# A spectral filter beside a token MLP: the first two pairs' step to token frequencies in one visit to the array's quarters

## Chip, cores and metric

The kernel runs on one core of one Trainium2 chip. The metric is the device time of one execution in microseconds; for the kernel before, the median of three runs is 366.05 us (365.9 to 366.07).

## The reference, cut to what matters

```python
x = A_x                                   # (1, 2048 tokens, 512 channels)
xn = layernorm(x)                         # over the channels
X = rfft2(xn) * (w_r + 1j * w_i)          # over tokens and channels
s = irfft2(X, (2048, 512))                # the global filter
u = gelu(einsum("bsd,sf->bdf", layernorm(xn), w1) + b1)    # w1: 2048 x 1792, over the tokens
y = einsum("bdf,fs->bds", u, w2) + b2
return x + s * silu(y.transpose(0, 2, 1))
```

All is float32. The large products (w1 and w2) are made of three products of rounded parts: each factor is split into a high part (a rounded copy) and a low part (the difference).

## The kernel before, in words

The work has three stages. In the first, the 16 blocks of 128 tokens are normalised, half of the hidden products are summed into six PSUM banks, and a first part of the token transform is written to `ey`, which holds its results by 16 low frequencies, `eyl(lo)`. In the second stage, which the change touches, TensorE goes through the rest of the hidden products (`hidden_rest`, rows `h..,w1e..` and `h..,w1h..`/`w1l..` of the profile), and between them through eight filter steps, each for a pair of low frequencies (`filter_pair`). In the third stage come the products with w2, the inverse transforms and the output.

One pair n goes through `filter_pair` in pieces, each ended by a `yield`:

1. load the table gf (`c_g[n]`);
2. and 3. twice: transform over the channels (rows `cd,ey`, four matmuls into bank 6 or 5), and a copy by ScalarE to `sh`, the pair's signals;
4. the way to token frequencies: four matmuls `sh,gf` of 64 rows into 64 columns, one in each quarter of the array (the profile shows two records for each matmul of this type, so eight), into banks 6 and 5; the load of hf (`c_h[n]`); two copies by ScalarE to `here`, a half of the tile `xc`; two transfers by GpSimd that write the other half, `there`, with the partitions swapped; and on GpSimd's queue two loads of filter weights `wt` (a ring of three buffers);
5. on VectorE: two small products `s1`, two scalings of 128x1024, four products of 128x512 with the weights;
6. on VectorE: a sum of 128x1024, two of 128x512, and a small one into `here` from `s1`;
7. the way back: 32 matmuls `hf,xc` in the array's quarters (64 records), which read `here`, and two copies to `ey`.

Which piece stands where among the hidden products is set in the loop over n at the end of the stage: `advance` takes a list in which a number is so many groups of hidden products (three matmuls each), `None` is a step that splits a part of the finished hidden layer (tiles `fa`, `fb`, `fc`, `fd`, `u`), and a pair of numbers `(k, piece)` takes the k-th of the filter generators one piece on. The order of pairs is `[1, 2, 0, 3, 4, 5, 6, 7]`: the first one's tiles carry the number 1 (`sh1`, `xc1`, `hf1`), the second's 2, the third's 0. In one such turn, pair n passes pieces 2 to 4, pair n-1 its VectorE work, and pair n-2 its way back just ahead of pair n's piece 4, so that two quarter steps are neighbours from the third pair on.

TensorE's matmuls and GpSimd's transfers keep the program's order. The order of the other engines is made when the program is built, by a list scheduler with the program's order as priority and costs of its own. Tiles of one tag share a ring of buffers; a load into one waits until its last reader is done. `w1_part` splits the hidden layer's weights (`w1s` into `w1h` on ScalarE and `w1l` on VectorE).

Of the kernel before, what the change touches and what calls it, by code (L numbers as in the profile page):

```python
# [9 lines left out]
F32 = mybir.dt.float32  # L10
F32R = mybir.dt.float32r
AF = mybir.ActivationFunctionType
# [3 lines left out]
P = 128  # L16
S, D, F = 2048, 512, 1792
# [124 lines left out]
def spectral_mixer_kernel(tc, x, w1, b1, w2, b2, wk, we, wx, c_f, c_ft, c_d, c_i, c_g, c_h, out):  # L142
    nc = tc.nc
    V, A, G, T, SY = nc.vector, nc.scalar, nc.gpsimd, nc.tensor, nc.sync

    def pool(stack, side, name, bufs):
        return stack.enter_context(tc.tile_pool(name=name, bufs=bufs, side=side, reuse_waits="tile"))
# [14 lines left out]
    with tc.tile_pool(name="ps", bufs=1, space=PSUM) as psp, ExitStack() as left, ExitStack() as right:  # L162
        ps = psp.tile([P, 8, 512], F32, name="ps")
# [161 lines left out]
        def w1_tiles(j):  # L325
            return [[w1r.tile([P, NE1 * P], F32R, name=f"w1{n}{a}_{j}", tag=f"w1{n}{a}", bufs=3) for n in "hl"] for a in range(2)]
# [134 lines left out]
        T = Kept(T, keep)  # L461
# [22 lines left out]
        w = w1_tiles(0)  # L484
# [23 lines left out]
        for j in range(NJ):  # L508
# [26 lines left out]
            if more:  # L535
                w = w1_tiles(j + 1)
# [84 lines left out]
        mp = pool(rstage, "right", "mid", 2)  # L621
# [9 lines left out]
        def eyl(lo):  # L631
            return ey.rearrange("p b (l h) j c -> p l b (h j c)", h=4)[:, lo]

        def filter_pair(n):

            gf = mp.tile([P, 2, 64], F32, name=f"gf{n}", tag="gf")
            SY.dma_start(gf, c_g[n])
            yield
            sh = []
            for l in range(2):  # L640
                pd = ps[:, 6 - l]
                for b in range(4):
                    T.matmul(pd[:, b * P:(b + 1) * P], eyl(2 * n + l)[:, b], cd[:, b], start=True, stop=True)
                sh.append(mp.tile([P, D], F32, name=f"sh{n}_{l}", tag="sh"))
                A.activation(sh[l], pd, AF.Copy)
                yield

            if n == 0:

                for l in range(2):  # L650
                    SY.dma_start(eyl(l)[:2], wx[:, 2 * l:2 * l + 2].rearrange("p k (b c) -> p (k b) c", c=P))
            for l in range(2):
                for t in range(2):
                    rows = slice(64 * t, 64 * t + 64)
                    T.matmul(ps[64 * l:64 * l + 64, 6 - t], gf[rows, l], sh[l][rows],
                             start=True, stop=True)

            hf = mp.tile([P, 2, 2, 64], F32, name=f"hf{n}", tag="hf")
            SY.dma_start(hf, c_h[n])


            xc = mp.tile([P, 2, 2, 2, 256], F32, name=f"xc{n}", tag="xc")
            there, here = xc[:, 0], xc[:, 1]
            for t in range(2):
                A.activation(here[:, :, t], ps[:, 6 - t].rearrange("p (s c) -> p s c", s=2), AF.Copy)  # L665
            for c in range(2):
                keep(G.dma_start(*(v.rearrange("p s t c -> p s (t c)") for v in (there[c::2], here[1 - c::2, ::-1]))))  # L667
            if n == 0:
                for to, signal, b in ((0, 0, 0), (1, 1, 1), (3, 0, 2), (2, 1, 2)):
                    V.tensor_mul(room(both, to), here[both, signal, 0].rearrange("p (h c) -> p h c", h=2), room(both, b))  # L670
            wt = wts.pop(), weights(2 * n + 1)
            if n != order[-1]:
                wts.append(weights(2 * order[order.index(n) + 1]))
            yield
            s1 = mp.tile([P, 2, 2, 2], F32, name=f"s1_{n}", tag="s1")
            k1, k2 = (e[:, 2 * n:2 * n + 2].rearrange("p t s -> p s t") for e in (e1, e2))
            V.tensor_mul(s1[:, 0], here[:, :, :, 0], k2)
            V.tensor_mul(s1[:, 1], there[:, ::-1, :, 0], k1)
            av, bv = (v.rearrange("p s t c -> p s (t c)") for v in (here, there))
            V.scalar_tensor_tensor(av, bv, turn[:, 0:1], av, op0=ALU.mult, op1=ALU.add)  # L680
            V.scalar_tensor_tensor(bv, bv, turn[:, 1:2], av, op0=ALU.mult, op1=ALU.subtract)
            for t in range(2):
                V.tensor_mul(here[:, :, t], here[:, :, t], wt[t][:, ::3])
                V.tensor_mul(there[:, :, t], there[:, :, t], wt[t][:, 1:3])
            yield
            V.tensor_add(there, there, here[:, ::-1])
            V.tensor_sub(here[:, 0], there[:, 1], there[:, 0])
            V.tensor_add(here[:, 1], there[:, 1], there[:, 0])
            V.tensor_add(here[:, :, :, 0], s1[:, 0], s1[:, 1])
            if n == 0:  # L690
                for s, op, (a, b) in ((0, V.tensor_sub, (0, 2)), (1, V.tensor_add, (1, 3))):
                    op(here[both, s, 0].rearrange("p (h c) -> p h c", h=2), room(both, a), room(both, b))
            yield

            po = [ps[:, bank].rearrange("p (b t c) -> p b t c", b=4, t=2) for bank in ((5, 6) if n == order[-2] else (3, 4))]
            for t in range(2):
                for b in range(4):
                    s = b // 2
                    for k in range(2):
                        c = 128 * (b % 2) + 64 * k  # L700
                        for l in range(2):
                            rows = slice(64 * l, 64 * l + 64)
                            T.matmul(po[l][64 * k:64 * k + 64, b, t], here[rows, s, t, c:c + 64], hf[rows, t, s],
                                     start=True, stop=True)
            for l in range(2):
                if n == order[-1]:
                    last_copies.append((eyl(2 * n + l), po[l].rearrange("p b t c -> p b (t c)")))
                else:
                    A.activation(eyl(2 * n + l), po[l].rearrange("p b t c -> p b (t c)"), AF.Copy)
            yield  # L710
# [3 lines left out]
        def room(rows, k):  # L714

            return eyl(k // 2)[rows, 2 * (k % 2):2 * (k % 2) + 2]

        def weights(i):
            wt = mp.tile([P, 4, 256], F32, name=f"wt{i}", tag="wt", bufs=WT)
            keep(G.dma_start(wt, wk[:, i]))  # L720
            return wt
# [5 lines left out]
        def form_step():  # L727

            while todo and held[0] + 2 <= passed[0]:
                if next(todo[0], "end") != "end":  # L730
                    return
                todo.pop(0)
# [29 lines left out]
        order = [1, 2, 0, 3, 4, 5, 6, 7]  # L762
        wts = [weights(2 * order[0])]
        filters = [filter_pair(n) for n in order]
        rest = hidden_rest()

        def advance(work):

            for what in work:
                if what is None:  # L770
                    form_step()
                elif isinstance(what, int):
                    for _ in range(what):
                        next(rest)
                else:
                    next(filters[what[0]])
# [8 lines left out]
        for n in range(8):  # L785
            a, b, c, d, e, f = PACE[n]
            u, v, w = ([None] * (k < MADE[n]) for k in range(3))
            advance([(n - 1, 5)] * (n > 0) + [(n, 1), a] + u + [(n, 2)] + [(n + 1, 0)] * (n < 7) + [b])
            advance([(n - 2, 6)] * (n > 1) + [(n, 3), c] + v + [d, (n, 4), e] + w + [f])
        advance([(7, 5), *LAST, (6, 6), (7, 6)])  # L790
        run(rest)
        passed[0] = NV + NJ
# [144 lines left out]
        V, A, SY, G = (Kept(e, keep) for e in (nc.vector, nc.scalar, nc.sync, nc.gpsimd))  # L937
# [209 lines left out]
```

## Time and profile before

| | |
|---|---|
| median of the runs | 366.05 us |
| the profiled execution | 366.06 us |
| its span, first to last instruction | 364.3 us |
| TensorE busy | 357.9 us, 98% |
| VectorE busy | 305.9 us, 84% |
| ScalarE busy | 211.2 us, 58% |
| GpSimd busy | 87.1 us, 24% |
| granted TensorE clock | 0.999 |

How to read it: PE is TensorE's matmuls, PEld its weight loads, DVE VectorE, ACT ScalarE, POOL GpSimd, SP SyncE. A row of the timeline has the start (us from the span's start), the length from the first start to the last end of the group, engine, line, operation, tiles out and in with their numbers left out, shape, count, and in brackets the idle time before it with what ended it. Matmuls overlap, so TensorE reads as busy throughout; a slower stage shows in the starts. A row of a queue (SPq, POOL with DMA) is the issue of transfers; when they land is told apart.

### The profile page before, as it was taken

To read this page: it belongs to the slowest core of one execution; us is meant where nothing else is said; L and a number is where in the kernel's file an instruction comes from. 1 tells how busy PE (TensorE), PEld (TensorE's weight loads), DVE (VectorE), ACT (ScalarE), POOL (GpSimd) and SP (SyncE) were. 2 spreads that over 40 slices of the span, in tenths; PEclk is the share of its full clock that TensorE was granted. 3 is DMA by queue.
4 is the path that set the end of the run, shared out by engine and by line. 5 is a ranking of instruction groups with operands and counts; after the bars stand their busy time and mean duration, and the time that the engine had idled before them with its cause. 6 is when DMAs were issued, how large, how long until landed. Compare 5 with 4: busy or idle time off the path is not lost.

```text
span 364.3 us, 8799 instructions
## 1 busy us (share of the span) xinstructions
PE 357.9 (98%) x3452; PEld 310.6 (85%) x3452; DVE 305.9 (84%) x587; ACT 211.2 (58%) x385; POOL 87.1 (24%) x134
## 2 busy tenths in 40 slices
PE   8999999999999999999999999999999999999994
PEld 7788888888777778777888999989898989898983
DVE  4899999967799996999995988687887969696984
ACT  3887788857534426755237875555464546565441
POOL 4233333323222012220111001040403223140330
PEclk9999999999999999999999999999999999999999
DMA  7978999306695596896568288688888989897724
GB/s 211 245 188 199 218 279 315 160 0 161 184 237 202 190 261 177 244 241 199 175 222 171 101 228 176 187 175 204 185 187 211 172 231 158 233 161 216 124 28 89
DMA packets 33293, 68.66 MB, mean 188 GB/s; under 512 B 4612, under 2 KB 19380, under 8 KB 33124
## 3 DMA queue, kind: packets, MB, share of 16 engines
q1 hardware_dynamic: 24276, 42.44, 42.0%
q0 software_dynamic: 8496, 25.01, 32.2%
q10 hardware_dynamic: 480, 0.66, 0.6%
q8 instruction: 27, 0.44, 0.5%
q14 instruction: 14, 0.11, 0.1%
HBM read 59.70 MB, written 8.13 MB: 186 GB/s over the span
## 4 chain that ended last, share of the span: by engine, by line
PE 97%; DMA 1%; ACT 0%; DVE 0%; ACTq 0%; issue 0%; DVEq 0%
PE ps L139 97%; DMA w1r<-in_w_dram 1%; DVE rows L139 0%; ACTq L452 0%; ACT w1h L466 0%; ACT g L139 0%; DVEq L1143 0%
## 5 line engine op out<-in xcount | busy, mean ns | idle before, releaser
L139 PE MATMUL ps<-h,w1h 128*128 128x512 f32 x400 | 116.5, 398 | 0.0
L139 PEld LDWEIGHTS ps<-h,w1h 128*128 128x128 f32 x400 | 72.9, 188 | 19.9 <-issue 4.9
L139 PE MATMUL ps<-h,w1l 128*128 128x512 f32 x200 | 67.6, 390 | 0.0
L139 DVE TENSOR_TENSOR w2f<-a,w2f 128x896 fp32r<-128x896 f32 x36 | 39.2, 1090 | 21.6 <-ACT w2f L139 21.6
L139 PEld LDWEIGHTS ps<-h,w1l 128*128 128x128 f32 x200 | 37.6, 188 | 8.1
L139 ACT ACTIVATE w2f<-a 128x896 fp32r<-128x896 f32 x36 | 36.8, 1023 | 12.8 <-PE ps L139 7.5
L139 PE MATMUL ps<-fb,w2f 128*128 128x256 f32 x336 | 41.9, 280 | 0.0
L139 POOL DMA_DIRECT2D s<-in_w_dram x14 | 18.4, 1311 | 96.1 <-DVE c L139 46.4
L139 PE MATMUL ps<-fa,w2f 128*128 128x256 f32 x336 | 41.3, 278 | 0.0
L139 PEld LDWEIGHTS ps<-fb,w2f 128*128 128x128 f32 x336 | 39.7, 188 | 0.9 <-issue 0.8
L139 PE MATMUL ps<-fc,w2f 128*128 128x256 f32 x336 | 39.9, 278 | 0.0
L139 PEld LDWEIGHTS ps<-fa,w2f 128*128 128x128 f32 x336 | 39.8, 188 | 0.0
L139 PEld LDWEIGHTS ps<-fc,w2f 128*128 128x128 f32 x336 | 39.2, 188 | 0.0
L139 POOL DMA_DIRECT2D out_dram<-r x28 | 23.6, 1278 | 27.5 <-DVE r L139 27.5
L155 ACT ACTIVATE w1h<-w1s 128x512 fp32r<-128x512 f32 x26 | 16.2, 632 | 23.7 <-PE ps L139 11.7
L667 POOL DMA_DIRECT2D xc<-xc x16 | 9.8, 620 | 70.3 <-ACT xc L665 55.1
L308 POOL TENSOR_TENSOR ey<-t 128x256 f32<-128x256 f32 x16 | 15.7, 978 | 44.0 <-DVE t L306 44.0
L139 ACT ACTIVATE w2f<-s 128x896 fp32r<-128x896 f32 x15 | 15.3, 1023 | 13.8 <-PE ps L139 12.4
L469 DVE TENSOR_TENSOR w1l<-w1r,w1h 128x384 fp32r<-128x384 f32 x32 | 21.3, 670 | 0.0
L139 PE MATMUL ps<-fd,w2f 128*128 128x256 f32 x168 | 20.7, 278 | 0.0
L139 ACT ACTIVATE g<-c,b2t 128x256 f32<-128x256 f32 x24 | 12.1, 505 | 14.6 <-DVE c L139 14.6
L268 ACT ACTIVATE h<-x,nbm,rsm 128x256 f32<-128x256 f32 (+1 forms) x34 | 18.4, 591 | 3.6 <-DVE nbm L263 3.0
(134 smaller groups left out, 605.7 us busy)
## 6 DMA issues: line engine op xcount, KB each, us to landing
a<-in_w_dram SPq DMA_DIRECT2D x22, 448.0 KB, 4.1
wt<-in_wk_dram POOLq DMA_DIRECT2D x16, 512.0 KB, 5.9
s<-in_w_dram SPq DMA_DIRECT2D x16, 448.0 KB, 4.5
s<-in_w_dram POOLq DMA_DIRECT2D x16, 448.0 KB, 6.8
w1s<-in_w_dram SPq DMA_DIRECT2D x52, 128.0 KB, 5.0
w1r<-in_w_dram SPq DMA_DIRECT2D x28, 192.0 KB, 4.7
xc<-xc POOLq DMA_DIRECT2D x16, 256.0 KB, 3.0
out_dram<-in_x_dram SPq DMA_DIRECT2D x4, 960.0 KB, 6.5
```

The costliest lines, as they stand in the source:

```text
L139: return lambda *args, **kw: self.keep(operation(*args, **kw))
L155: return A.activation(hi, src, AF.Copy), V.tensor_sub(lo, src, hi.bitcast(F32))
L268: keep(A.activation(to, v, AF.Identity, bias=m["nb"][:, i], scale=m["rs"][:, i, 1:2]))
L308: G.tensor_add(ey[:, 0::3, :, j], a, b)
L469: keep(V.tensor_sub(dst, src, hi.bitcast(F32)))
L667: keep(G.dma_start(*(v.rearrange("p s t c -> p s (t c)") for v in (there[c::2], here[1 - c::2, ::-1]))))
```

## The change

The first pair's visit to the quarters is taken away from its place, and its four matmuls stand in one visit with the second pair's, at the second pair's place. Its signals stay meanwhile in a buffer of tag xc (`shs`) in place of two of tag sh, and its results go to banks 4 and 3 in place of 6 and 5. What follows on the visit (copies, transfers, weight loads, VectorE's pieces) moves with it: the first pair's piece 5 stands after the second pair's visit, piece 6 ahead of the third pair's first channel transform, side by side with the second pair's piece 5. The way back of the first pair stays where it was.

```diff
+            top = 4 if n == order[0] else 6
...
-            sh = []
+            sh, first = [], n == order[0]
+            if first:
+                shs = mp.tile([P, 2, 2, 2, 256], F32, name=f"shs{n}", tag="xc")
...
-                sh.append(mp.tile([P, D], F32, name=f"sh{n}_{l}", tag="sh"))
+                sh.append(shs[:, 0, l].rearrange("p s c -> p (s c)") if first else mp.tile([P, D], F32, name=f"sh{n}_{l}", tag="sh"))
...
-                    T.matmul(ps[64 * l:64 * l + 64, 6 - t], gf[rows, l], sh[l][rows],
+                    T.matmul(ps[64 * l:64 * l + 64, top - t], gf[rows, l], sh[l][rows],
...
-                A.activation(here[:, :, t], ps[:, 6 - t].rearrange("p (s c) -> p s c", s=2), AF.Copy)
+                A.activation(here[:, :, t], ps[:, top - t].rearrange("p (s c) -> p s c", s=2), AF.Copy)
...
-            advance([(n - 1, 5)] * (n > 0) + [(n, 1), a] + u + [(n, 2)] + [(n + 1, 0)] * (n < 7) + [b])
-            advance([(n - 2, 6)] * (n > 1) + [(n, 3), c] + v + [d, (n, 4), e] + w + [f])
+            advance([(0, 5)] * (n == 2) + [(n - 1, 5)] * (n > 1) + [(n, 1), a] + u + [(n, 2)] + [(n + 1, 0)] * (n < 7) + [b])
+            if n < 2:
+                advance([(0, 3)] * n + v + [(0, 4), (1, 3)] * n + [c, d] + [(1, 4)] * n + [e] + w + [f])
+            else:
+                advance([(n - 2, 6), (n, 3), c] + v + [d, (n, 4), e] + w + [f])
```

In the code the pieces count from 0: `(k, 3)` is piece 4 of the list above, `(k, 6)` the way back.

TensorE at the two visits, before (in the rows a tile's name carries the pair's or block's number, and last a buffer number):

```order
L139 MATMUL ps_58<-h1_83,w1e1_1018 128x512 x6
L139 MATMUL ps_58<-sh1_0_1418,gf1_1387 64x512 x2
L139 MATMUL ps_58<-sh1_1_1433,gf1_1387 64x512 x2
L139 MATMUL ps_58<-h2_84,w1e2_1109 128x512 x12
L139 MATMUL ps_58<-h3_85,w1e3_1166 128x512 x9
```
```order
L139 MATMUL ps_58<-h4_86,w1e4_1241 128x512 x6
L139 MATMUL ps_58<-sh2_0_1513,gf2_1435 64x512 x2
L139 MATMUL ps_58<-sh2_1_1536,gf2_1435 64x512 x2
L139 MATMUL ps_58<-h4_86,w1e4_1241 128x512 x3
```

and the same two places now:

```order
L139 MATMUL ps_58<-h1_83,w1e1_1018 128x512 x6
L139 MATMUL ps_58<-h2_84,w1e2_1109 128x512 x12
L139 MATMUL ps_58<-h3_85,w1e3_1166 128x512 x9
```
```order
L139 MATMUL ps_58<-h4_86,w1e4_1241 128x512 x6
L139 MATMUL ps_58<-shs1_1414,gf1_1387 64x512 x4
L139 MATMUL ps_58<-sh2_0_1484,gf2_1434 64x512 x2
L139 MATMUL ps_58<-sh2_1_1507,gf2_1434 64x512 x2
L139 MATMUL ps_58<-h4_86,w1e4_1241 128x512 x3
```

The first visit is gone, and the second holds both pairs; nothing else moves on TensorE.

VectorE at the end of the first pair's work, before: from the four products with the weights (wt2, wt3) to the small piece from s1, which is the last that the way back of pair 1 waits for.

```order
L683 TENSOR_TENSOR xc1_1449<-xc1_1449,wt2_1385 128x2x256
L684 TENSOR_TENSOR xc1_1449<-xc1_1449,wt2_1385 128x2x256
L683 TENSOR_TENSOR xc1_1449<-xc1_1449,wt3_1454 128x2x256
L684 TENSOR_TENSOR xc1_1449<-xc1_1449,wt3_1454 128x2x256
L686 TENSOR_TENSOR xc1_1449<-xc1_1449 128x1024
L677 TENSOR_TENSOR s1_2_1584<-xc2_1552,e2_68 128x4
L368 TENSOR_TENSOR fd1_1633<-u1_1360,fd1_1633 128x256
L687 TENSOR_TENSOR xc1_1449<-xc1_1449 128x512
L688 TENSOR_TENSOR xc1_1449<-xc1_1449 128x512
L689 TENSOR_TENSOR xc1_1449<-s1_1_1477 128x4
```

The same now, from the first scaling to the products, and from there to the small piece:

```order
L681 TENSOR_TENSOR s1_1_1539<-xc1_1523,e1_67 128x4
L683 SCALAR_TENSOR_TENSOR xc1_1523<-xc1_1523,cft_63 128x1024
L684 SCALAR_TENSOR_TENSOR xc1_1523<-xc1_1523,cft_63 128x1024
L368 TENSOR_TENSOR fa1_2135<-u1_1360,fa1_2135 128x2x256
L686 TENSOR_TENSOR xc1_1523<-xc1_1523,wt2_1385 128x2x256
L687 TENSOR_TENSOR xc1_1523<-xc1_1523,wt2_1385 128x2x256
L686 TENSOR_TENSOR xc1_1523<-xc1_1523,wt3_1528 128x2x256
L687 TENSOR_TENSOR xc1_1523<-xc1_1523,wt3_1528 128x2x256
L393 TENSOR_TENSOR u1_1360<-u1_1360 128x256
```
```order
L689 TENSOR_TENSOR xc1_1523<-xc1_1523 128x1024
L681 TENSOR_TENSOR s1_2_1579<-xc2_1554,e1_67 128x4
L683 SCALAR_TENSOR_TENSOR xc2_1554<-xc2_1554,cft_63 128x1024
L690 TENSOR_TENSOR xc1_1523<-xc1_1523 128x512
L684 SCALAR_TENSOR_TENSOR xc2_1554<-xc2_1554,cft_63 128x1024
L691 TENSOR_TENSOR xc1_1523<-xc1_1523 128x512
L686 TENSOR_TENSOR xc2_1554<-xc2_1554,wt4_1530 128x2x256
L687 TENSOR_TENSOR xc2_1554<-xc2_1554,wt4_1530 128x2x256
L686 TENSOR_TENSOR xc2_1554<-xc2_1554,wt5_1559 128x2x256
L687 TENSOR_TENSOR xc2_1554<-xc2_1554,wt5_1559 128x2x256
L692 TENSOR_TENSOR xc1_1523<-s1_1_1539 128x4
L155 TENSOR_TENSOR w1l10_1644<-w1s10_1493,w1h10_1643 128x512
```

Two scalings and four products of the second pair now stand ahead of the first pair's last small piece.

ScalarE between the signals and the copies of the visits, before and now:

```order
L363 ACTIVATE fa0_1571<-u0_1356 128x2x256
L155 ACTIVATE w1h6_1486<-w1s6_1390 128x512
L155 ACTIVATE w1h7_1518<-w1s6_1390 128x512
L665 ACTIVATE xc1_1449<-ps_58 128x2x256 x2
L155 ACTIVATE w1h8_1564<-w1s8_1395 128x512
L155 ACTIVATE w1h9_1596<-w1s8_1395 128x512
L363 ACTIVATE fc0_1608<-u0_1356 128x2x256
L645 ACTIVATE sh2_0_1513<-ps_58 128x512
L363 ACTIVATE fb0_1611<-u0_1356 128x2x256
L645 ACTIVATE sh2_1_1536<-ps_58 128x512
L665 ACTIVATE xc2_1552<-ps_58 128x2x256 x2
```
```order
L363 ACTIVATE fa0_1532<-u0_1356 128x2x256
L363 ACTIVATE fc0_1603<-u0_1356 128x2x256
L648 ACTIVATE sh2_0_1484<-ps_58 128x512
L363 ACTIVATE fb0_1606<-u0_1356 128x2x256
L648 ACTIVATE sh2_1_1507<-ps_58 128x512
L155 ACTIVATE w1h6_1461<-w1s6_1390 128x512
L155 ACTIVATE w1h7_1489<-w1s6_1390 128x512
L668 ACTIVATE xc1_1523<-ps_58 128x2x256 x2
L155 ACTIVATE w1h8_1566<-w1s8_1395 128x512
L155 ACTIVATE w1h9_1591<-w1s8_1395 128x512
L668 ACTIVATE xc2_1554<-ps_58 128x2x256 x2
```

The splitting of w1s6 and the first pair's copies now stand behind the second pair's signals. On GpSimd's queue the order is unchanged (xc1, wt3, wt4, xc2, wt5, wt0), on SyncE's gf0 and the loads of w1s10 now stand ahead of hf1.

## The prediction

> **What bounds the kernel now.** I read the page first, then the chain of waits, then the instructions of TensorE, ScalarE, GpSimd and VectorE in order of time between 83 and 124 us, where the edit lies, and last the landing times of the transfers there.
>
> ```profile
> span 364.3 us, 8799 instructions
> PE 357.9 (98%) x3452; PEld 310.6 (85%) x3452; DVE 305.9 (84%) x587; ACT 211.2 (58%) x385; POOL 87.1 (24%) x134
> PE 97%; DMA 1%; ACT 0%; DVE 0%; ACTq 0%; issue 0%; DVEq 0%
> ```
>
> TensorE carries 97% of the chain that ends last. So two things count: array time taken away, and any moment at which TensorE has to stand still. The profiled execution took 366.06 us, its span 364.3 and 1.76 around it; the median of the runs is 366.05, so I sum against 366.06.
>
> TensorE around the edit (start, length, instruction, count; lengths overlap, so I use differences of starts):
>
> ```profile
> 83.49 2.88 PE L139 MATMUL ps<-h,w1e 128*128 128x512 f32 x12
> 86.21 1.05 PE L139 MATMUL ps<-cd,ey 128*128 128x128 f32 x8
> ...
> 89.28 1.62 PE L139 MATMUL ps<-h,w1e 128*128 128x512 f32 x6
> 90.83 1.09 PE L139 MATMUL ps<-sh,gf 64*64 64x512 f32 x8
> 91.85 5.07 PE L139 MATMUL ps<-h,w1e 128*128 128x512 f32 x21
> ...
> 101.39 1.09 PE L139 MATMUL ps<-sh,gf 64*64 64x512 f32 x8
> 102.41 3.71 PE L139 MATMUL ps<-h,w1e 128*128 128x512 f32 x15
> 105.96 0.62 PE L139 MATMUL ps<-h,w1h 128*128 128x512 f32 x2
> ...
> 111.94 1.16 PE L139 MATMUL ps<-hf,xc 64*64 64x64 f32 x64
> 112.92 1.04 PE L139 MATMUL ps<-sh,gf 64*64 64x512 f32 x8
> 113.89 0.72 PE L139 MATMUL ps<-h,w1h 128*128 128x512 f32 x2
> ```
>
> The two rows sh,gf at 90.83 and 101.39 are the two visits that become one. The row hf,xc at 111.94 is what the first pair's signals are for: its way back. It begins 21 us after the first visit. After the change the visit is the second one, and 10 us are left. Everything turns on whether the filter's work fits into them.
>
> **The saving.** Twelve matmuls of the hidden layer take 86.21-83.49 = 2.72 us, 0.227 each. Six from 89.28 would end at 90.64; so without the first visit the next work starts at 90.64 in place of 91.85: 1.21 us sooner. The second visit starts at 101.39-1.21 = 100.18 and now holds twice the matmuls. What the pair that joins costs no row shows directly: the nearest is the visit at 112.92, which joins quarters already in use and takes 113.89-112.92 = 0.97, leaving them included; the least is that less one switch of the array, if leaving the quarters costs what entering them does, 90.83-90.64 = 0.19: 0.78. I take 0.85. The saving is 1.21-0.85 = 0.36 us (ends 0.24 and 0.43), and hf,xc would be due at 111.94-0.36 = 111.58.
>
> **What is moved with the visit.** First the rows, ScalarE, GpSimd and SyncE, then VectorE:
>
> ```profile
> 91.93 1.15 ACT L155 ACTIVATE w1h<-w1s 128x512 fp32r<-128x512 f32 x2 [0.36 <-DMA w1s<-in_w_dram]
> 92.99 1.07 ACT L665 ACTIVATE xc<-ps 128x512 f32<-128x512 f32 x2
> ...
> 102.53 1.09 ACT L665 ACTIVATE xc<-ps 128x512 f32<-128x512 f32 x2 [1.75 <-PE ps L139]
> ```
> ```profile
> 94.64 1.23 POOL L667 DMA_DIRECT2D xc<-xc  x2 [8.27 <-issue]
> 95.86 1.11 POOL L720 DMA_DIRECT2D wt<-in_wk_dram  x2
> 103.91 1.23 POOL L667 DMA_DIRECT2D xc<-xc  x2 [6.93 <-ACT fd L363]
> ```
> ```profile
> 95.52 2.60 SPq L197 DMA_DIRECT2D w1s<-in_w_dram  x4
> ```
> ```profile
> 94.20 1.29 DVE L155 TENSOR_TENSOR w1l<-w1s,w1h 128x512 fp32r<-128x512 f32 x2
> ...
> 98.86 0.16 DVE L678 TENSOR_TENSOR s<-xc,e 128x4 f32<-128x4 f32 x1 [1.50 <-DMA xc<-xc]
> 98.94 1.28 DVE L680 SCALAR_TENSOR_TENSOR xc<-xc,cft 128x1024 f32<-128x1024 f32 x1
> 100.14 0.68 DVE L368 TENSOR_TENSOR fb<-u,fb 128x512 fp32r<-128x512 f32 x1
> 100.74 1.28 DVE L681 SCALAR_TENSOR_TENSOR xc<-xc,cft 128x1024 f32<-128x1024 f32 x1
> 102.05 0.69 DVE L683 TENSOR_TENSOR xc<-xc,wt 128x512 f32<-128x512 f32 x1
> ...
> 104.59 1.22 DVE L686 TENSOR_TENSOR xc<-xc 128x1024 f32<-128x1024 f32 x1
> 105.73 0.16 DVE L677 TENSOR_TENSOR s<-xc,e 128x4 f32<-128x4 f32 x1
> ...
> 106.14 0.68 DVE L687 TENSOR_TENSOR xc<-xc 128x512 f32<-128x512 f32 x1
> ...
> 107.46 0.17 DVE L689 TENSOR_TENSOR xc<-s 128x4 f32<-128x4 f32 x1
> ...
> 108.26 0.42 DVE L393 TENSOR_TENSOR u<-u 128x256 f32<-128x256 f32 x1
> ...
> 110.61 0.17 DVE L678 TENSOR_TENSOR s<-xc,e 128x4 f32<-128x4 f32 x1 [0.55 <-DMA xc<-xc]
> ```
>
> Landing times, of all xc transfers and of all wt loads, and of hf loads between 80 and 130 us (size, median):
>
> ```profile
> DMA to landing us min/median/max: 2.3/3.0/6.0
> ```
> ```profile
> DMA to landing us min/median/max: 4.1/5.9/8.4
> ```
> ```profile
> hf<-in_c_h_dram SPq DMA_DIRECT2D x4, 128.0 KB, 4.0
> ```
>
> *Edits that cost nothing, and their cover.* The copies of the first pair's signals (shs) are the same two in another buffer. ScalarE now splits w1h6 and w1h7 after the second pair's signals, and VectorE w1l6 and w1l7 after them: the second copy of those signals is needed by the visit at 100.18, so the four end by about 100.2 + 1.29 = 101.5, and their matmuls (the row at 105.96) come at 105.60: 4 us of cover. The w1s10 loads, which SyncE issued at 95.52, just after the first w1l pair ended, go out about 6 us later for that; they feed h10, whose matmuls stand behind the visit at 112.92. gf0 now waits for the visit's last reader of gf1, and hf1 stands behind gf0 on SyncE: issued near 105.5, landed 4.0 later near 109.5, before 111.58. If that cover fails, hf1 takes the wait, but the next chain is far later.
>
> *The chain that isn't covered.* Visit at 100.18. The copies of the second pair began 102.53-101.39 = 1.14 after their visit; the same for the first pair gives 101.32, and two copies (1.09) end at 102.41. GpSimd issued at 103.91, 0.29 after the copies' end: now 102.70, the second half at 103.32. Landing: 2.3 to 6.0, so 105.6 to 109.3. The first pair's own transfer in the before run met idle queues (VectorE got it at 98.86), the second pair's met w1s and wt loads and VectorE waited until 110.61. After the change it comes with w1s10 just ahead of it and wt behind it, between the two: I take 4.25, that is 107.6.
>
> Then VectorE, in the order of the rows shown in the section on the change, by start-to-start times from the rows above. s 0.08; first scaling 1.31 (100.74 to 102.05, the next one depends on it); second 1.20 (98.94 to 100.14); fa1 0.60 (like fb, 100.14 to 100.74); four products with the weights 2.54 (102.05 to 104.59); u1 0.42; the sum of 128x1024 1.14; pair 2's s 0.08; **pair 2's first scaling 1.20**; the first 128x512 sum 0.60; **pair 2's second scaling 1.20**; the second sum 0.60; **pair 2's four products 2.54**; and last the first pair's small piece xc1<-s1, 0.17. Together 13.7 us, of which 4.9 belong to pair 2. In the before run the same piece of work took 107.63-98.86 = 8.8 with fb and fd between. The last piece ends at 107.6+13.7 = 121.3. TensorE's hf,xc reads what it writes, so it starts at 121.4 and not at 111.58: TensorE, whose matmuls stand in a fixed order, pauses for 9.8 us. Against before the row moves by 121.4-111.94 = **9.46 us**, the saving included.
>
> Two loads inside that chain could be later still. wt5 takes wt2's buffer, so it is issued after the first two products (107.6+3.19+1.27 = 112.1, GpSimd some 0.3 later) and lands 4.1 to 8.4 after, 116.5 to 120.8; its products are due at 119.9: nothing to 0.9 more, I take nothing. xc2 follows wt3 and wt4 on GpSimd's queue (1.11 us): issued until 106.3, landed by 112.3 at the longest row, due at 114.9: nothing, and if the 1 MB ahead of it adds 3 us or more, it shows.
>
> *The clock.* After so long a pause the array starts slowly. Rows of the start, of the same shape in the last stage, and of the end of the span (column two of the last: TensorE's busy time; the number after the bracket: granted clock):
>
> ```profile
> L139 PE MATMUL ps<-wz 128*128 128x256 f32 x18 | 4.2, 423 | 1.1 <-POOL wz L443 1.1
> ```
> ```profile
> L139 PE MATMUL ps<-fb,w2f 128*128 128x256 f32 x29 | 3.7, 280 | 0.0
> ```
> ```profile
> 363.00:364.30 1.30, 0.00 (x0) 0.69 0.00 0
> ```
>
> The first row is the stretch from 1.6 to 5.0 us: a matmul of 128x256 takes 423 ns at the start against 280 warm, for about 4 us from the first one (1.1 us). The last row says that the clock fell to half 0.8 us before the span's end, 363.5, that is 3.8 us after the last matmul. The pause of 9.8 is longer than 3.8. So I count 4 us of half clock after it, 2.0 us lost if all of it were array time; the first 64 small matmuls may hide some: 1.8, between 0 and 3.4.
>
> By the Trainium skill ("TensorE: Matmul & The Clock Gate", Part 1) the gate closes after an idle window of about 3.4 us and opens after a busy one, and the windows run freely, so 3.4 to 6.8 us at half clock; by that the loss would be 1.7 to 3.4 us and the time 377.2 to 378.9. The trace's 3.8 and 4 us agree with it as far as they go; no run here shows a pause in mid-kernel.
>
> Afterwards nothing more is lost: pair 2's last piece follows some 4 us after pair 1's, at 125, and TensorE wants it 11.5 us after hf1 (the spacing of the visits); everything later finds VectorE further ahead than before. Nothing is given back either, as TensorE had no other waits to fill.
>
> **Sum:** 366.06 + 9.46 + 1.8 = **377.3 us**.
>
> **Rivals.**
> - *No stall (the other side).* The edit saves its 0.36 us: 365.7. For it: TensorE is the chain and never waited for a pair. Against: it would need xc1's last piece by 111.58, so a landing by 97.9 with the order built, or 102.8 with the 8.8 us of before; the visit itself begins at 100.18. It decides only if the work isn't as I read it. 0.05.
> - *Short stall.* VectorE gets through pair 1 in the 8.8 us of before because pair 2's pieces cost less there or pair 1's data is early: 107.6+8.8+0.1-111.94 = 4.6, with 1.8 for the clock 372.4. The order speaks against it, pair 2's products stand ahead of xc1<-s1. 0.08.
> - *Clock stays up,* stall as forecast: 366.06+9.46 = 375.5. Against it stands the row at 363 us. 0.10.
> - *Longer stall.* All loads meet (w1s10, xc1, wt3, wt4, xc2, w1s12 between 101 and 108 us): landing at 109.3, wt5 0.9 late, clock 2.5: 366.06+9.46+1.7+0.9+2.5 = 380.6. For it: the 6.0 and 8.4 in the landing rows. 0.15.
> - *The forecast,* 0.62, with its own range 374.5 to 380.0: landing 105.6 to 109.3 moves it by 2.0 and 1.7 us, the clock by the rest.
>
> **How the numbers follow.** The time is the forecast's. The range 373.0 to 381.0 holds the forecast, the clock rival and most of the longer stall; left out are no stall, short stall and the far end of the longer one, under 0.2 together. About 0.2% (0.7 us) can be told from no change here. No stall gives 365.7, inside it: same 0.04, faster 0.02 if the saving were twice as large. All else is slower, 0.94.
>
> **What would show it.** Right: one sh,gf group of 16 records near 100.2 and none near 90.8; then an idle time of 8 to 12 us before hf,xc, released by VectorE's small xc<-s; the granted clock near half for some 4 us behind it; pair 2's products before that xc<-s on VectorE. Wrong: hf,xc near 111.6 without idle time; a wait that DMA hf ends; the lost time in another place, or a second pause before the next hf,xc. The prediction fails most easily in the landing time of xc1 and in the length of VectorE's chain.

## The result, and the profile after

The changed kernel takes 378.01 us (median of five runs, 377.52 to 380.48) against 366.05 before: a ratio of 1.0342, 95% interval 1.0321 to 1.0363. The profiled execution took 378.00 us, its span 376.2; the differences below are against the 366.06 and 364.3 of before.

The page and its chain of waits:

```profile
span 376.2 us, 8801 instructions
PE 359.5 (96%) x3452; PEld 312.0 (83%) x3452; DVE 306.3 (81%) x587; ACT 211.4 (56%) x385; POOL 87.1 (23%) x134
PE 91%; DMA 4%; DVE 2%; issue 1%; POOL 1%; ACT 0%; DVEq 0%; POOLq 0%; ACTq 0%
```

The engines work as long as before (TensorE 1.6 us longer), the span has 11.9 us more. The chain is no longer TensorE alone: a transfer and VectorE have a share. In order of time, the transfer on it is pair 2's second one, on its way until 116.04:

```profile
105.74 10.30 DMA xc<-xc
```

One row of before that was not shown yet serves as a landmark, the second channel transform ahead of both visits:

```profile
88.48 1.05 PE L139 MATMUL ps<-cd,ey 128*128 128x128 f32 x8
```

TensorE after the change:

```profile
88.38 1.05 PE L139 MATMUL ps<-cd,ey 128*128 128x128 f32 x8
...
100.03 1.09 PE L139 MATMUL ps<-shs,gf 64*64 64x512 f32 x8
100.93 1.04 PE L139 MATMUL ps<-sh,gf 64*64 64x512 f32 x8
101.90 3.69 PE L139 MATMUL ps<-h,w1e 128*128 128x512 f32 x15
...
111.10 0.39 PE L139 MATMUL ps<-h,w1l 128*128 128x512 f32 x1
122.43 1.99 PE L139 MATMUL ps<-hf,xc 64*64 64x64 f32 x64 [10.94 <-DVE xc L692]
124.19 1.73 PE L139 MATMUL ps<-sh,gf 64*64 64x512 f32 x8
125.85 0.73 PE L139 MATMUL ps<-h,w1h 128*128 128x512 f32 x2
```

From the landmark to the work behind the second visit it was 102.41-88.48 = 13.93 us and is 101.90-88.38 = 13.52: the saving is real, 0.41 us. Then TensorE has nothing to do for 10.94 us, and what ends it is VectorE's small piece at line 692. From the landmark to hf,xc it was 23.46 and is 34.05, 10.59 more. The two groups behind the pause take 125.85-122.43 = 3.42 us in place of 113.89-111.94 = 1.95, 1.47 more. 10.59+1.47 = 12.06, less 0.10 that this execution was ahead at the landmark, is 11.96; the two profiled executions differ by 11.94. So nothing of weight is lost or given back elsewhere.

What leads to that piece: ScalarE, GpSimd, and VectorE after the change.

```profile
101.17 1.09 ACT L668 ACTIVATE xc<-ps 128x512 f32<-128x512 f32 x2 [0.77 <-PE ps L139]
```
```profile
102.84 1.23 POOL L670 DMA_DIRECT2D xc<-xc  x2 [16.56 <-issue]
104.07 1.10 POOL L723 DMA_DIRECT2D wt<-in_wk_dram  x2
105.14 1.25 POOL L670 DMA_DIRECT2D xc<-xc  x2
113.07 0.55 POOL L723 DMA_DIRECT2D wt<-in_wk_dram  x1 [6.68 <-DVE xc L687]
```
```profile
108.28 0.16 DVE L681 TENSOR_TENSOR s<-xc,e 128x4 f32<-128x4 f32 x1 [3.25 <-DMA xc<-xc]
108.36 1.28 DVE L683 SCALAR_TENSOR_TENSOR xc<-xc,cft 128x1024 f32<-128x1024 f32 x1
...
114.22 1.22 DVE L689 TENSOR_TENSOR xc<-xc 128x1024 f32<-128x1024 f32 x1
116.13 0.16 DVE L681 TENSOR_TENSOR s<-xc,e 128x4 f32<-128x4 f32 x1 [0.69 <-DMA xc<-xc]
116.21 1.28 DVE L683 SCALAR_TENSOR_TENSOR xc<-xc,cft 128x1024 f32<-128x1024 f32 x1
...
118.01 1.28 DVE L684 SCALAR_TENSOR_TENSOR xc<-xc,cft 128x1024 f32<-128x1024 f32 x1
...
119.80 0.69 DVE L686 TENSOR_TENSOR xc<-xc,wt 128x512 f32<-128x512 f32 x1
...
121.61 0.69 DVE L687 TENSOR_TENSOR xc<-xc,wt 128x512 f32<-128x512 f32 x1
122.21 0.17 DVE L692 TENSOR_TENSOR xc<-s 128x4 f32<-128x4 f32 x1
```

VectorE stood idle for 3.25 us for pair 1's transfer, began at 108.28, and put pair 2's wait, scalings and products (116.13 and after) between pair 1's sums and its last piece. In the trace before that piece ended at 107.63; here at 122.38.

The landing times of the transfers, the two of pair 1 and then the two of pair 2:

```profile
DMA to landing us min/median/max: 3.9/4.3/4.7
```
```profile
DMA to landing us min/median/max: 9.7/10.0/10.3
```

### The profile page after: what moved, and what is told of

Read it like the earlier page. It is cut to its first block, busy times and chain, and to the rows that moved or that the text cites. A ratio compares the mean times of both kernels' runs of the same rounds, so it can differ in the third digit from the quotient of the medians.

```text
span 376.2 us, 8801 instructions
## 1 busy us (share of the span) xinstructions
PE 359.5 (96%) x3452; PEld 312.0 (83%) x3452; DVE 306.3 (81%) x587; ACT 211.4 (56%) x385; POOL 87.1 (23%) x134
## 4 chain that ended last, share of the span: by engine, by line
PE 91%; DMA 4%; DVE 2%; issue 1%; POOL 1%; ACT 0%; DVEq 0%; POOLq 0%; ACTq 0%
PE ps L139 91%; DMA xc<-xc 3%; DMA x<-in_x_dram 1%; DVE xc L687 0%; DVE xc L684 0%; DVE xc L683 0%; POOL xc L670 0%; POOL wt L723 0%; DVE rows L139 0%; DVE stm L244 0%; DVE w1l L155 0%; DVE xc L686 0%; ACT w1h L155 0%; DVE xc L691 0%; ACT xc L668 0%
## 5 line engine op out<-in xcount | busy, mean ns | idle before, releaser
L155 DVE TENSOR_TENSOR w1l<-w1s,w1h 128x512 fp32r<-128x512 f32 x26 | 17.7, 688 | 7.7 <-ACT w1h L155 7.6
```

The source lines that it names most:

```text
L155: return A.activation(hi, src, AF.Copy), V.tensor_sub(lo, src, hi.bitcast(F32))
```

## The experiments

### Is it the short time, or the merged visit itself?

The early merged visit keeps both pairs in one visit but puts it where the first visit stood; pair 2's channel transforms move forward for that.

```diff
-            advance([(0, 5)] * (n == 2) + [(n - 1, 5)] * (n > 1) + [(n, 1), a] + u + [(n, 2)] + [(n + 1, 0)] * (n < 7) + [b])
-            if n < 2:
-                advance([(0, 3)] * n + v + [(0, 4), (1, 3)] * n + [c, d] + [(1, 4)] * n + [e] + w + [f])
-            else:
-                advance([(n - 2, 6), (n, 3), c] + v + [d, (n, 4), e] + w + [f])
+            if n == 0:
+                advance([(0, 1), a] + u + [(0, 2), (1, 0), b, (1, 1), c] + v + [(1, 2), d, (0, 3), (1, 3), e, (0, 4)] + w + [f])
+            elif n == 1:
+                advance([(0, 5), a] + u + [(2, 0), b, c] + v + [d, (1, 4), e] + w + [f])
+            else:
+                advance([(n - 1, 5), (n, 1), a] + u + [(n, 2)] + [(n + 1, 0)] * (n < 7) + [b])
+                advance([(n - 2, 6), (n, 3), c] + v + [d, (n, 4), e] + w + [f])
```

> The merged visit is kept, but it stands where the first visit stood (a little later, near 95 us), for which the second pair's channel transforms are moved forward. Theory (one visit saves 0.4 us, the loss is only the short time left for pair 1's filter work): hf,xc of pair 1 starts near 111.4 without idle time, the clock stays at 1, time 365.6 us. Rival 1 (the saving isn't real, a visit of twice the matmuls takes as long as two): 366.05. Rival 2 (VectorE can't do both pairs' work side by side whatever the time left): an idle time of some us before hf,xc, 369 us or more.

Measured: 365.57 us (11 runs), before on the same chip 365.84; ratio 0.9992, interval 0.9983 to 1.0000. Its TensorE (landmark at 88.32, the same row):

```profile
88.32 1.05 PE L139 MATMUL ps<-cd,ey 128*128 128x128 f32 x8
...
95.21 1.09 PE L139 MATMUL ps<-shs,gf 64*64 64x512 f32 x8
96.12 1.04 PE L139 MATMUL ps<-sh,gf 64*64 64x512 f32 x8
...
111.36 1.16 PE L139 MATMUL ps<-hf,xc 64*64 64x64 f32 x64
112.34 1.41 PE L139 MATMUL ps<-sh,gf 64*64 64x512 f32 x8
113.68 0.72 PE L139 MATMUL ps<-h,w1h 128*128 128x512 f32 x2
```

The way back comes 111.36-88.32 = 23.04 us after the landmark, 0.42 sooner than before, without idle time. So the 12 us don't come with the merged visit as such: rival 2 is out, and rival 1 is out by these rows, not by the time, whose interval reaches 1. The place alone isn't shown to be enough: this list also puts pair 1's piece 6, `(0, 5)`, ahead of pair 2's piece 5, `(1, 4)`, so place and order change together, and the part of the order is measured two experiments on. The next visit takes 113.68-112.34 = 1.34 us in place of 0.97, and 0.37 of the 0.42 is gone again. ScalarE shows what stood in the way: the splitting of w1s10 waits for its load, and the third pair's second signals stand behind it.

```profile
111.50 0.63 ACT L155 ACTIVATE w1h<-w1s 128x512 fp32r<-128x512 f32 x1 [3.01 <-DMA w1s<-in_w_dram]
```

### The early visit with ScalarE's order mended

In the early visit with the signals first, ScalarE's two instructions are held in the program's order.

```diff
-                A.activation(sh[l], pd, AF.Copy)
+                copy = A.activation(sh[l], pd, AF.Copy)
+                if n == order[2]:
+                    keep(copy)
...
-            split(wh, wl, w)
+            halves = split(wh, wl, w)
+            if i == 10:
+                keep(halves[0])
```

> As the early merged visit, with one more edit: ScalarE copies the third pair's second signals ahead of w1h10, which there waited 3.0 us for its load and held the visit after hf,xc back (1.34 us between its start and the next work, in place of 0.97). Theory (that wait ate the saving): the visit takes 0.97 again, the second way back starts 36.8 us after the first channel transform (37.22 before, 37.17 in the early visit), time 0.4 us under the kernel before. Rival (the 0.37 us goes elsewhere, the visit is long because quarters are entered with both kinds of matmuls): no change against the early visit, 0.1 to 0.2 us under the kernel before.

Measured: 365.48 us (11 runs) against 366.00; ratio 0.9986, interval 0.9977 to 0.9995.

```profile
112.21 1.04 PE L139 MATMUL ps<-sh,gf 64*64 64x512 f32 x8
113.18 0.72 PE L139 MATMUL ps<-h,w1h 128*128 128x512 f32 x2
```

The visit takes 0.97 again, the second way back starts 122.72-85.92 = 36.80 us after the first channel transform, as the theory had it, and the saving stays. This is the fastest version: 0.5 us (0.14%) under the kernel before, and 12.5 under the change.

### How much of the pause is VectorE's order?

The pinned order holds VectorE's filter work of the two pairs in a fixed order, pair 1's piece 6 ahead of pair 2's piece 5; every VectorE instruction of pieces 5 and 6 goes through `W`. (In the change's list pair 1's piece 5, `(0, 4)`, already stands ahead of pair 2's visit, `(1, 3)`, and not behind it; only piece 6 stands behind pair 2's piece 5.)

```diff
-            advance([(0, 5)] * (n == 2) + [(n - 1, 5)] * (n > 1) + [(n, 1), a] + u + [(n, 2)] + [(n + 1, 0)] * (n < 7) + [b])
+            advance([(n - 1, 5)] * (n > 1) + [(n, 1), a] + u + [(n, 2)] + [(n + 1, 0)] * (n < 7) + [b])
-                advance([(0, 3)] * n + v + [(0, 4), (1, 3)] * n + [c, d] + [(1, 4)] * n + [e] + w + [f])
+                advance([(0, 3)] * n + v + [(0, 4), (1, 3)] * n + [c, d] + [(0, 5), (1, 4)] * n + [e] + w + [f])
...
+            W = Kept(V, keep) if n in order[:2] else V
...
-            V.tensor_mul(s1[:, 0], here[:, :, :, 0], k2)
+            W.tensor_mul(s1[:, 0], here[:, :, :, 0], k2)
...
```

> The changed kernel with VectorE's filter work of the first two pairs in a fixed order: all of pair 1's pieces first, then pair 2's. Theory (4.9 us of pair 2's work and the 0.7 us wait for its transfer stand ahead of pair 1's last piece): from the landing at 108.3 the rest is 9.4 us, hf,xc starts near 117.8 in place of 122.4, time 373.4 us with the clock still falling. Rival (the late transfer alone is it, the order is hidden behind other waits): hf,xc at 122.4, 378.0. Neither: below 368, which would mean that the order alone was the loss.

Measured: 373.59 us (4 runs), ratio 1.0202, interval 1.0182 to 1.0221. VectorE and TensorE:

```profile
107.87 0.17 DVE L139 TENSOR_TENSOR s<-xc,e 128x4 f32<-128x4 f32 x1 [2.92 <-DMA xc<-xc]
...
117.09 0.16 DVE L139 TENSOR_TENSOR xc<-s 128x4 f32<-128x4 f32 x1
```
```profile
117.31 1.99 PE L139 MATMUL ps<-hf,xc 64*64 64x64 f32 x64 [5.89 <-DVE xc L139]
```

The last piece ends 9.4 us after the landing in place of 14.1, and the pause falls from 10.94 to 5.89 us. Of these 5 us, 4.7 are pair 2's work and its transfer's wait, which no longer stand ahead; 0.3 is pair 1's transfer, which VectorE had that much sooner after the landmark (107.87-88.30 in place of 108.28-88.38). The other 5.9 remain with VectorE's order mended: pair 1's copies, transfer and VectorE work, with 1.9 us of other small VectorE work still between its pieces, do not fit into the 10 us left.

The milder form changes the list of pieces alone (the first four lines of that diff) and leaves VectorE's order to the scheduler.

> The changed kernel with pair 1's piece 6 written ahead of pair 2's piece 5, and the order on VectorE left to the scheduler: pair 2's products then stand behind pair 1's last piece, but its two scalings ahead of it. Theory (VectorE waits in its order, so pair 2's transfer, landed at 116.1, stays a wait of pair 1): hf,xc near 120.0, time 375.6. Rival (only the amount of work ahead counts: 2.5 us of products less and no wait): 119.3 or below, 374.9.

A single run: 374.84 us.

```profile
115.56 0.16 DVE L681 TENSOR_TENSOR s<-xc,e 128x4 f32<-128x4 f32 x1 [0.52 <-DMA xc<-xc]
...
119.24 0.16 DVE L692 TENSOR_TENSOR xc<-s 128x4 f32<-128x4 f32 x1
```
```profile
119.45 1.99 PE L139 MATMUL ps<-hf,xc 64*64 64x64 f32 x64 [8.18 <-DVE xc L692]
```

The wait for pair 2's transfer still stands ahead of pair 1's last piece, as the theory has it; from its end to hf,xc it took 119.45-115.56 = 3.89 us, and 3.9 were forecast (116.1 to 120.0). The time is the rival's, since VectorE had the transfer 0.6 us sooner than in the run it was reckoned from, and the two groups behind the pause took 3.24 us in place of 3.42. The time alone could not tell the two apart; the row with its wait does, in this one run.

### Is the slow restart the clock?

The filled pause has 44 matmuls ahead of pair 1's hf,xc, into a bank that hf,xc overwrites.

```diff
+            if n == order[0]:
+                for _ in range(44):
+                    T.matmul(ps[:, 3], hh[0][:, :P], hh[0], start=True, stop=True)
```

> The changed kernel with 44 matmuls of 128x512 (0.227 us each, 10.0 us) on TensorE just ahead of pair 1's hf,xc, into a PSUM bank that hf,xc overwrites; their result is not used. They fill the pause of 10.9 us. Theory (the half clock after the pause costs 1.47 us: hf,xc 1.76 instead of 0.98, sh,gf 1.66 instead of 0.97): hf,xc still starts near 122.4, the granted clock stays at 1, time 376.5 us. Rival (the first matmuls after the pause are slow for another reason, a queue that has to fill): 378.0, hf,xc still 1.8 us long.

Measured: 376.81 us (4 runs), ratio 1.0299, interval 1.0283 to 1.0315.

```profile
111.25 10.13 PE L139 MATMUL ps<-h 128*128 128x512 f32 x44
122.71 1.16 PE L139 MATMUL ps<-hf,xc 64*64 64x64 f32 x64 [1.32 <-DVE xc L692]
123.69 1.04 PE L139 MATMUL ps<-sh,gf 64*64 64x512 f32 x8
124.66 0.73 PE L139 MATMUL ps<-h,w1h 128*128 128x512 f32 x2
```

With the array kept at work the two groups take 1.95 us as before, though hf,xc still waits for VectorE. The rival had 1.8 us for hf,xc alone; it took 0.98. The time falls by 1.2 us and not by 1.47, since hf,xc came 0.36 us later after the landmark (122.71-88.30 = 34.41). The granted clock of the changed kernel, in stretches cut at its edges (the column after TensorE's busy time and count), shows the same from the other side:

```profile
111.50:115.34 3.84, 0.00 (x0) 1.00 1.09 308
115.35:122.40 7.05, 0.00 (x0) 0.50 0.50 158
122.43:125.58 3.15, 3.15 (x72) 0.50 0.04 8
125.59:128.00 2.41, 2.41 (x13) 1.00 0.27 78
```

### Why did pair 2's transfer land after 10 us?

In the kernel with the loads later, GpSimd issues both pairs' transfers first and wt3, wt4 behind them.

```diff
-            wt = wts.pop(), weights(2 * n + 1)
-            if n != order[-1]:
-                wts.append(weights(2 * order[order.index(n) + 1]))
+            if n == order[1]:
+                early.append((wts.pop(), weights(2 * order[0] + 1)))
+                wts.append(weights(2 * n))
+            if n != order[0]:
+                wt = wts.pop(), weights(2 * n + 1)
+                ...
```

> The changed kernel with GpSimd issuing both pairs' transfers first and the weight loads wt3 and wt4 (1 MB) behind them; the scheduler orders VectorE anew, so the time is no measure. Theory (a transfer lands late because it stands behind 1 MB of loads on its queue): pair 2's transfer, issued about 1 us sooner, lands 5 to 6 us after its issue in place of 9.7 to 10.3; pair 1's transfer lands as before, 3.9 to 4.7. Rival (the DMA engines are full with SyncE's loads whatever the queue's order): still 8 us or more.

A single run: 378.37 us. The landing times of pair 2's two transfers:

```profile
DMA to landing us min/median/max: 4.5/4.9/5.3
```

Halved, with SyncE's loads issued as they were: the rival is out, and it was the megabyte issued ahead on GpSimd's queue. Whether the place in the queue or the DMA engines shared with that megabyte makes the difference isn't separated. The time doesn't fall: wt3 now lands about 1 us later, and the scheduler put still more of pair 2's work ahead of pair 1's last piece.

### The neutral parts

The buffers alone: the kernel before with `shs` and banks 4 and 3, both visits in their old places (the change's diff up to the lists of pieces).

> The kernel before, with two parts of the change alone: pair 1's signals in a buffer of tag xc, and the visit's results in banks 4 and 3. Both visits stand where they stood. Theory (both parts cost nothing): 366.05 us, no wait before hf,xc. Rival (the xc buffer that the signals hold makes pair 2's transfer wait, or bank 4 or 3 is still read): slower by 0.5 us or more.

Measured: 365.86 us (10 runs) against 365.84; ratio 0.9998, interval 0.9987 to 1.0009. Its hf,xc starts 23.46 us after the landmark, as before. They cost nothing.

## Why the prediction was right, point by point

- **The saving**, 0.36 us: measured 0.41 and, in the early visit, 0.42. Within its ends (0.24 and 0.43).
- **The edits with cover:** none ended a wait of TensorE, and the buffers cost nothing. But hf1's cover did not hold: a landing near 109.5 was reckoned, 4.0 us after the issue, before the 111.58 at which hf,xc was due. Issued at 104.48, it landed at 112.5 by the updates of its semaphore in the trace, 8.0 us later, and hf2, issued right behind it, took 10.2. It stayed hidden only because VectorE came later still; with VectorE's work done in time, hf,xc would have waited about 1 us for hf1. The four loads behind that 4.0 held one of 7.5 already. That nothing was right for this term was luck.
- **Pair 1's transfer**, landing at 107.6: VectorE had it at 108.28. 4.25 us from the second issue was taken, a choice between two rows and not worked out; 4.7 came.
- **VectorE's chain**, 13.7 us: 14.1, of which 0.69 was a wait that the sum had at nothing. The step that was mis-sized is xc2's landing, "nothing, and if the 1 MB ahead of it adds 3 us or more, it shows": it added 4 us (10.3 in place of the longest 6.0), and it showed. The experiment with the loads later ties it to the megabyte issued ahead.
- **wt5** was issued at 113.07, after the first two products, and no wait for it shows: the nothing was right.
- **hf,xc** moved by 10.59 us where 9.46 were forecast: 0.7 for pair 1's landing and 0.7 for that wait, less 0.3 that the instructions themselves were shorter. Against these 1.1 us too little stands the clock, 0.3 too much; so 377.3 came within 0.7 of 378.0 with errors that partly cancel.
- **The clock**, 1.8 us: 1.47 by the rows behind the pause, which the filled pause confirms (two groups of 1.95 us in place of 3.42). It fell 3.9 us after the last matmul (115.35) and rose 3.15 us after the first (125.58), where 3.8 and 4 were taken. The Trainium skill's idle window of about 3.4 us ("TensorE: Matmul & The Clock Gate", Part 1) agrees with the fall, 3.9 us after the last matmul; the loss of 1.7 to 3.4 us, an estimate from its windows, was above the measured 1.47, as the clock rose 3.15 us after work began, sooner than one whole window.
- **Afterwards** nothing was lost or returned: the sum of the two local terms is the whole difference within 0.02 us.
- **The rivals:** no stall and a short stall are out by the row with 10.94 us; the clock that stays up is out by the row with 0.50; the longer stall had the right mechanism (loads that meet), but they cost 1.4 us (0.7 at each pair's transfer) and wt5 nothing, where it had 1.7 and 0.9, and its clock of 2.5 us was 1.47.

## What to carry to other kernels

Moving a producer later saves nothing until one has counted the way from it to its reader on every engine and queue between: here 0.4 us of array time were bought with 10 us of a 21 us lead, and the way took 22, and 17 with VectorE's order mended. Count the loads on that way too: hf1 landed 8 us after its issue where 4 had been seen. On an engine that works in order, look what the new program puts *ahead* of the last small instruction that a bound engine waits for: 4.7 of the 11 us were another pair's work and the wait for its transfer. And merge at the earlier of the two places if the later one's inputs can be brought forward; that, with pair 1's pieces listed first, kept the saving, once a copy no longer stood behind an instruction that waits for a load.

## What the runs showed of the hardware

The half-clock stretch of the pinned order is as long as two thirds of the change's, though its pause is little more than half as long, and most of it lies in the work behind the pause: 

```profile
111.50:116.01 4.51, 0.00 (x0) 1.00 1.10 307
116.02:122.84 6.82, 5.54 (x77) 0.50 0.49 166
```

The change's stretch is 125.58-115.35 = 10.23 us, this one 6.82: three and two times 3.41. The two single runs, the milder form and the loads later, have the same two lengths:

```profile
115.43:122.24 6.81, 2.79 (x72) 0.50 0.46 156
```
```profile
115.81:126.03 10.22, 3.40 (x72) 0.50 0.25 80
```

So the clock changes on a grid of 3.41 us that doesn't follow the pause: it fell 3.9, 4.6, 4.1 and 4.5 us after the last matmul in these four runs (the change, the pinned order, the milder form, the loads later). What the pause costs depends on where in the grid work begins again. In the change it began 0.26 us into a window of the grid (122.43, the window from 125.58-3.41 = 122.17), and the clock rose at that window's end. In the pinned order it began 1.29 us into one (117.31, from 116.02), and the clock rose only a whole window later. So a pause of 5.9 us left 5.5 us of work at half clock, and one of 10.9 left 3.15: a shorter pause can cost more of the clock than a longer one. The Trainium skill ("TensorE: Matmul & The Clock Gate", Part 1) gives such a window, 3413 ns and free-running; the four stretches agree with it. Whether the grid is also behind the wider spread of the changed kernel's runs (377.52 to 380.48, 3 us, against 0.9 in five runs of the kernel before) isn't shown: their mean granted clocks, 0.982 to 0.986, don't go with their times throughout (0.985 at 378.96, 0.984 at 377.52).
